# Pinning the early steps of a weight conversion to program order on ScalarE and VectorE

## The chip, the cores and the metric

The kernel runs on one core of a Trainium2 chip, as one launch. The metric is the device time of that launch in microseconds (us), the median of several executions.

## The reference

Sliding-window attention with sinks (2 batches, 8 heads, 768 positions, head size 64), followed by two feed-forward blocks over the 1536 tokens, each with d_model 512 and d_ff 2048. Only the activations differ. The weights of both blocks are 64-bit floats.

```
scores = where(is_sink | in_window, scale * q @ k.T, -1e9)      # 4 sinks, window 128
a = exp(scores - max); a = a / (sum(a) + 1e-9);  x = a @ v      # per batch and head
h = x @ w_in;  g = where(h >= 1, h, where(h <= -1, 0, (h + 1)**2 / 4));  x = g @ w_out
h = x @ w2_in; g = h * clip(h + 3, 0, 6) / 6;                   return g @ w2_out
```

## The kernel before

The program has an attention part and then, for each feed-forward block m, a first half over 16 d_ff tiles and a second half over the held activations.

**Attention.** `pairs` runs over four groups of query blocks (`GROUPS`) and four head pairs, so there are 16 pairs. Pairs 0 to 3 take four query blocks of 128 rows each, pairs 4 to 7 two, pairs 8 to 11 two (blocks 0 and 1 of the second batch), pairs 12 to 15 four. A unit is one query block of one pair; `score` makes its scores on TensorE (L310), VectorE adds the mask and finds the row minimum of the negated scores (L317), ScalarE takes exponentials (L336), VectorE makes the reciprocal of the sum (L328, L329), and GpSimd scales the two rows of probabilities (L331, two instructions a unit). `turn` transposes them on TensorE (L371, L372) and ScalarE or VectorE copies them out of PSUM (L353, L355). `sinks` does the same for the sink columns (L383), and `mix` multiplies by v (L408) once a pair, writing the feed-forward's input as a high and a low part (`xh`, `xl`).

**Weights.** `load_w` brings a weight tile of 128 x 512 doubles (512 KB) into one of four `raw` buffers by a DMA on SyncE (L162). Tiles are named by block, kind and d_ff tile: raw0i0 is w_in of block 0, tile 0; raw0o1 is w_out, tile 1. `take_weight` calls `take`, which calls `narrow` to make 32-bit floats in a tile w32 of the two halves of each double, and then `split` into a high and a low part (`wi`, `wo`). The steps of `narrow`:

- the high word without its sign, on ScalarE (L176) or VectorE (L174), whichever the planner `Balance` picks
- a clamp on VectorE (L179)
- the sign of the high word, in place in raw, on VectorE (L180)
- shift and join, on VectorE (L181)
- the low word to a float, in place in raw, on ScalarE (L184)
- one slot later, the sum of both on VectorE (L186)

Two slots later the high part is made (L134 on ScalarE or L136 on VectorE), then the low part on VectorE (L141). L174 or L176, L180 and L184 read nothing but what the DMA brought; the others read a step before them. `load_weights` issues the next load when a tile has been taken, three slots later, and that load waits for its raw buffer.

**Order.** TensorE and SyncE run in the order of the program text (`manual_schedule`). For ScalarE, VectorE and GpSimd the compiler's scheduler, which simulates a timeline, chooses the order in which instructions stand on each engine; on the chip each engine then takes them strictly in that order, waiting on semaphores. The program text loads the first four weight tiles half way through the attention's steps and takes raw0i0, raw0o0 and raw0i1 24, 14 and 6 steps before its end; all others are taken in the feed-forward part.

**Feed-forward, first half.** For each d_ff tile, `h_group` does 12 matmuls for each of three token chunks (L534) and `y_group` 12 for chunk 0 of the tile before (L564). `activate` works on chunk 0 at once: r on ScalarE (L511), then two steps on VectorE (L512, L513), then gh (L134) and gl (L141). Chunks 1 and 2 are held as copies `hs` (L134). PSUM has four `ps_h` buffers.

Of the kernel before, what the change touches and what calls it, by code (L numbers as in the profile page):

```python
# [11 lines left out]
U32 = mybir.dt.uint32  # L12
AF = mybir.ActivationFunctionType
ALU = mybir.AluOpType
# [51 lines left out]
def f32(ap):  # L66
    return ap.bitcast(F32)
# [3 lines left out]
def sink_attention_moe_moe_kernel(  # L71
# [14 lines left out]
    nc = tc.nc  # L86
# [27 lines left out]
    def defer(fn, slots=1):  # L114
        waiting.append((clock[0] + slots, fn))
# [14 lines left out]
    def high(dst, src, n, psum=False):  # L130

        e = bal.pick(act=(143 if psum else 190) + n / 1.2, dve=(140 + n / 0.96) if psum else (150 + n / 1.92))
        if e == "act":
            nc.scalar.activation(out=dst, in_=src, func=AF.Copy)  # L134
        else:
            nc.vector.tensor_copy(out=dst, in_=src)  # L136

    def low(dst, src, hi, n):

        bal.add("dve", 150 + n / 0.96)  # L140
        nc.vector.tensor_tensor(out=dst, in0=src, in1=f32(hi), op=ALU.subtract)  # L141
# [23 lines left out]
            nc.sync.dma_start(out=t, in_=src)  # L165
        raw[m, which, fc] = t

    def narrow(t, dst):

        lo, hi = t[:, :, 0], t[:, :, 1]  # L170
        c = dst.bitcast(I32)
        n = c.shape[1]
        if bal.pick(dve=150 + n / 1.92, act=150 + n / 1.2) == "dve":
            nc.vector.tensor_scalar(out=c, in0=hi, scalar1=0x7FFFFFFF, scalar2=None, op0=ALU.bitwise_and)  # L174
        else:
            nc.scalar.activation(out=f32(c), in_=f32(hi), func=AF.Abs)  # L176
        bal.add("dve", 3 * 150 + 2 * n / 1.92 + n / 0.96)
        bal.add("act", 150 + n / 1.2)
        nc.vector.tensor_scalar(out=f32(c), in0=f32(c), scalar1=F64_LOW, scalar2=F64_HIGH, op0=ALU.max, op1=ALU.min)  # L179
        nc.vector.tensor_scalar(out=hi, in0=hi, scalar1=-(1 << 31), scalar2=None, op0=ALU.bitwise_and)  # L180
        nc.vector.scalar_tensor_tensor(  # L181
            out=c, in0=c, scalar=3, in1=hi, op0=ALU.logical_shift_left, op1=ALU.bitwise_xor
        )
        nc.scalar.activation(out=f32(lo), in_=lo.bitcast(U32), func=AF.Copy, scale=2.0 ** -51, bias=2.0)  # L184
        bal.add("dve", 160 + 1.3 * n)
        defer(lambda: nc.vector.tensor_tensor(out=c, in0=c, in1=lo, op=ALU.add))  # L186

    def take(m, which, fc):

        t = raw.pop((m, which, fc))  # L190
        if which == "i":
            w = wi_p.tile([P, 2, DM], F32R, tag="wi", name=f"wi{m}")
            hi, lo = w[:, 0, :], w[:, 1, :]
            wi[m, fc] = (hi.rearrange("p (k f) -> p k f", f=P), lo.rearrange("p (k f) -> p k f", f=P))
        else:
            w = wo_tile(m, fc)
            hi, lo = w[:, 0, :], w[:, 1, :]

        def split(src):
            high(hi, src, DM)  # L200
            defer(lambda: low(lo, src, hi, DM))
            if which == "o":
                defer(lambda: nc.sync.dma_start(out=f32(wo_d[m][fc]), in_=f32(w.rearrange("p a f -> p (a f)"))), 4)

        if wide:
            t32 = raw_p.tile([P, DM], F32, tag="w32", name="w32", bufs=3)
            narrow(t, t32)
            defer(lambda: split(t32), 2)
        else:
            split(t)  # L210

    def wo_tile(m, fc):
        wo[m, fc] = wo_p.tile([P, 2, DM], F32R, tag="wo", name=f"wo{m}")
        return wo[m, fc]
# [372 lines left out]
    def take_weight(m, which, fc):  # L587
        if taken[0] < len(queue) and queue[taken[0]] == (m, which, fc):
            take(m, which, fc)
            taken[0] += 1  # L590
            defer(load_weights, 3)
# [3 lines left out]
    with tc.manual_schedule(engines={mybir.EngineType.PE, mybir.EngineType.SP}):  # L595
# [28 lines left out]
        for m in range(2):  # L624
# [19 lines left out]
            for n, (_, fc, c) in enumerate(first):  # L644
# [3 lines left out]
                if n + 2 < len(first):  # L648
                    t = held.pop(first[n + 2])
# [51 lines left out]
```

## Time and profile before

| what | us |
|---|---|
| median of 3 runs (654.04 to 656.28) | 655.56 |
| the profiled execution, its own time | 655.16 |
| its span in the trace | 653.4 |
| TensorE busy | 630.7 |
| VectorE busy | 423.2 |
| ScalarE busy | 328.2 |
| GpSimd busy | 91.5 |

The span runs from the first to the last instruction; the time of a launch has about 1.8 us around it. A matmul is pipelined and its end is modelled, so TensorE's busy time also covers stretches in which it is not at its peak. An engine's idle time is shown with what ended it.

### The profile page before, as it was taken

The numbers are of one execution on the slowest core, as the hardware profiler recorded it, in microseconds if no ns is written. First come the engines' busy times: TensorE is split into PE (matmuls) and PEld (weight loads), VectorE is DVE, ScalarE is ACT, GpSimd is POOL, SyncE is SP. The second block draws the span as 40 slices with busy tenths as digits, with TensorE's granted clock in tenths as the row PEclk, the third lists the DMA queues.
The fourth block names the chain that finished last, engine by engine and source line by source line (L and its number), as shares of the span: only waits on it lengthen the run. The fifth ranks groups of instructions, "written<-read, shape, count | busy, mean of one in ns | idle before, by whom it ended". The sixth has DMA issues, their size and how long they took to land.

```text
span 653.4 us, 8514 instructions
## 1 busy us (share of the span) xinstructions
PE 630.7 (97%) x3008; PEld 493.6 (76%) x3008; DVE 423.2 (65%) x953; ACT 328.2 (50%) x669; POOL 91.5 (14%) x115
## 2 busy tenths in 40 slices
PE   7997797899999999999999999999999999999997
PEld 4554454588888887888888888888888888888886
DVE  4778888856647567539995597565668302994443
ACT  5777679655455445337663486455533223850001
POOL 7896687200000000000000000000000000000000
PEclk9999799899999999999999999999999999999999
DMA  4237257734453344102223575445451010523203
GB/s 129 88 115 247 70 167 233 229 107 141 129 161 129 115 144 128 65 32 97 98 96 118 174 236 182 162 129 161 129 158 68 34 64 1 192 98 96 97 32 130
DMA packets 32330, 81.38 MB, mean 125 GB/s; under 512 B 3056, under 2 KB 12320, under 8 KB 32288
## 3 DMA queue, kind: packets, MB, share of 16 engines
q1 hardware_dynamic: 32288, 80.84, 38.1%
q8 instruction: 24, 0.39, 0.3%
q14 instruction: 18, 0.15, 0.1%
HBM read 60.91 MB, written 19.92 MB: 124 GB/s over the span
## 4 chain that ended last, share of the span: by engine, by line
PE 72%; DVE 10%; DMA 9%; ACT 6%; issue 2%; POOL 1%; SPq 0%; ACTq 0%; POOLq 0%; DVEq 0%
PE ps_y L564 36%; PE ps_h L534 28%; DMA raw0o<-moe_w_out_dram 6%; PE ps_v L408 3%; PE ps_s L310 3%; DVE w L186 2%; DVE w L181 2%; DMA raw0i<-moe_w_in_dram 2%; ACT p L336 1%; PE ps_t L371 1%; ACT w L176 1%; ACT raw0o L184 1%; DVE w L179 1%; PE ps_t L372 1%; DVE r L512 1%
## 5 line engine op out<-in xcount | busy, mean ns | idle before, releaser
L534 PE MATMUL ps_h<-xh,wi 128*128 128x512 f32 x768 | 242.1, 390 | 0.0
L564 PE MATMUL ps_y<-gh,wo 128*128 128x512 f32 x768 | 241.6, 389 | 0.0
L534 PEld LDWEIGHTS ps_h<-xh,wi 128*128 128x128 f32 x768 | 144.5, 188 | 30.3 <-issue 0.3
L564 PEld LDWEIGHTS ps_y<-gh,wo 128*128 128x128 f32 x768 | 144.1, 188 | 29.9
L564 PE MATMUL ps_y<-gl,wo 128*128 128x512 f32 x384 | 149.6, 390 | 0.6 <-DVE gl L141 0.6
L534 PE MATMUL ps_h<-xl,wi 128*128 128x512 f32 x384 | 149.6, 390 | 0.0
L331 POOL TENSOR_SCALAR p<-p,sm 128x260 f32<-128x260 f32 (+2 forms) x96 | 88.1, 938 | 25.7 <-DVE sm L329 8.6
L564 PEld LDWEIGHTS ps_y<-gl,wo 128*128 128x128 f32 x384 | 72.1, 188 | 16.2 <-DVE gl L141 1.3
L534 PEld LDWEIGHTS ps_h<-xl,wi 128*128 128x128 f32 x384 | 72.2, 188 | 15.0
L179 DVE TENSOR_SCALAR w<-w 128x512 f32<-128x512 f32 x64 | 27.7, 433 | 43.9 <-ACT w L176 42.9
L134 ACT ACTIVATE hs<-ps_h 128x512 f32<-128x512 f32 x64 | 37.5, 589 | 36.4 <-PE ps_h L534 36.3
L336 ACT ACTIVATE p<-p,nm 128x260 f32<-128x260 f32 (+2 forms) x96 | 46.3, 483 | 15.0 <-DVE nm L317 11.4
L141 DVE TENSOR_TENSOR gl<-hs,gh 128x512 fp32r<-128x512 f32 x64 | 44.0, 688 | 12.7 <-ACT gh L134 11.9
L310 PE MATMUL ps_s<-kraw,qraw 64*128 64x260 f32 (+2 forms) x192 | 37.8, 469 | 7.8 <-DMA kraw<-k_dram 4.4
L512 DVE SCALAR_TENSOR_TENSOR r<-r 128x512 f32<-128x512 f32 x48 | 32.3, 685 | 15.6 <-ACT r L511 15.4
L141 DVE TENSOR_TENSOR wi<-w,wi 128x512 fp32r<-128x512 f32 x32 | 22.1, 690 | 30.6 <-ACT wi L134 29.6
L516 DVE SCALAR_TENSOR_TENSOR ps_h<-r,ps_h 128x512 f32<-128x512 f32 x16 | 11.1, 694 | 46.2 <-ACT r L515 46.2
L317 DVE CUSTOM_DVE_ANT_0 p<-ps_s,mask 128x260 f32<-128x260 f32 (+2 forms) x96 | 35.7, 396 | 7.7 <-PE ps_s L310 7.0
L134 ACT ACTIVATE gh<-ps_h 128x512 fp32r<-128x512 f32 x32 | 19.2, 598 | 33.6 <-DVE ps_h L513 21.7
L134 ACT ACTIVATE gh<-hs 128x512 fp32r<-128x512 f32 x35 | 22.0, 629 | 26.0 <-PE ps_y L564 24.8
L572 ACT ACTIVATE o<-ps_y 128x512 f32<-128x512 f32 x6 | 3.6, 596 | 62.5 <-PE ps_y L564 62.5
L136 DVE CAST gh<-hs 128x512 fp32r<-128x512 f32 x29 | 12.3, 426 | 32.8 <-PE ps_y L564 32.7
(72 smaller groups left out, 688.7 us busy)
## 6 DMA issues: line engine op xcount, KB each, us to landing
wo_d<-wo SPq DMA_DIRECT2D x32, 512.0 KB, 5.0
wo<-wo_d SPq DMA_DIRECT2D x32, 512.0 KB, 3.2
raw0i<-moe_w_in_dram SPq DMA_DIRECT2D x16, 512.0 KB, 3.4
raw0o<-moe_w_out_dram SPq DMA_DIRECT2D x16, 512.0 KB, 5.1
raw1i<-moe_w_in_dram SPq DMA_DIRECT2D x16, 512.0 KB, 3.4
raw1o<-moe_w_out_dram SPq DMA_DIRECT2D x16, 512.0 KB, 4.1
out_dram<-o SPq DMA_DIRECT2D x12, 256.0 KB, 2.2
qraw<-q_dram SPq DMA_DIRECT2D x8, 256.0 KB, 2.8
```

The lines of the kernel that those rows point to most:

```text
L134: nc.scalar.activation(out=dst, in_=src, func=AF.Copy)
L141: nc.vector.tensor_tensor(out=dst, in0=src, in1=f32(hi), op=ALU.subtract)
L179: nc.vector.tensor_scalar(out=f32(c), in0=f32(c), scalar1=F64_LOW, scalar2=F64_HIGH, op0=ALU.max, op1=ALU.min)
L181: nc.vector.scalar_tensor_tensor(out=c, in0=c, scalar=3, in1=hi, op0=ALU.logical_shift_left, op1=ALU.bitwise_xor)
L310: nc.tensor.matmul(banks[e], tq[rows, u * P:(u + 1) * P], tk[rows, c0:c0 + w], start=True, stop=True)
L317: nc.vector.tensor_tensor_reduce(out=p[:, e, :], in0=banks[e], in1=masks[min(i, 2)], scale=-SCALE, scalar=BIG, op0=ALU.add, op1=ALU.min, a ...
L331: nc.gpsimd.tensor_scalar_mul(out=p[:, e, :], in0=p[:, e, :], scalar1=sm[:, e:e + 1])
L336: nc.scalar.activation(out=p[:, e, :], in_=p[:, e, :], func=AF.Exp, scale=-1.0, bias=nm[:, e:e + 1], accum_out=sm[:, e:e + 1],)
L408: nc.tensor.matmul(ps[e * D:(e + 1) * D, u0 * P:u1 * P], l, r, start=n == 0, stop=n == len(ops[0]) - 1)
L512: nc.vector.scalar_tensor_tensor(out=r, in0=r, scalar=1.0, in1=r, op0=ALU.min, op1=ALU.mult)
L534: nc.tensor.matmul(ps, w[:, kc, :], x[:, kc, :], start=i == 0, stop=i == len(ops) - 1)
L564: nc.tensor.matmul(ys[dm], a[:, cs], b, start=fc == 0 and i == 0, stop=last and i == 2)
```

## The change

`narrow` gets a third argument. For block 0 and d_ff tiles 0 to 2, the three steps that depend on the load alone are handed to `keep_in_program_order`, which adds an edge in the scheduler's graph from the instruction that was traced just before on the same engine: the step must stand behind it. The edge is of issue order only; no wait on a semaphore is added. No instruction is added or removed, and the planner's picks of engine stay as they are.

```diff
-    def narrow(t, dst):
+    def narrow(t, dst, keep):
+
+        def place(ins):
+            if keep:
+                tc.keep_in_program_order(ins)
 
         lo, hi = t[:, :, 0], t[:, :, 1]
...
         if bal.pick(dve=150 + n / 1.92, act=150 + n / 1.2) == "dve":
-            nc.vector.tensor_scalar(out=c, in0=hi, scalar1=0x7FFFFFFF, scalar2=None, op0=ALU.bitwise_and)
+            place(nc.vector.tensor_scalar(out=c, in0=hi, scalar1=0x7FFFFFFF, scalar2=None, op0=ALU.bitwise_and))
         else:
-            nc.scalar.activation(out=f32(c), in_=f32(hi), func=AF.Abs)
+            place(nc.scalar.activation(out=f32(c), in_=f32(hi), func=AF.Abs))
...
-        nc.vector.tensor_scalar(out=hi, in0=hi, scalar1=-(1 << 31), scalar2=None, op0=ALU.bitwise_and)
+        place(nc.vector.tensor_scalar(out=hi, in0=hi, scalar1=-(1 << 31), scalar2=None, op0=ALU.bitwise_and))
...
-        nc.scalar.activation(out=f32(lo), in_=lo.bitcast(U32), func=AF.Copy, scale=2.0 ** -51, bias=2.0)
+        place(nc.scalar.activation(out=f32(lo), in_=lo.bitcast(U32), func=AF.Copy, scale=2.0 ** -51, bias=2.0))
...
-            narrow(t, t32)
+            narrow(t, t32, m == 0 and fc < 3)
```

The order of TensorE, SyncE and GpSimd is the same in both programs. After the change all lines of the program from `narrow` on stand four to five lines further down (L184 is L188, L511 is L515).

First place: ScalarE in pair 8, just after the first four weight loads have been issued. The names p, pt, pts and ps_t belong to attention, raw0i0 and raw0o0 are weight tiles. Before:

```order
L353 ACTIVATE pt_877<-ps_t_925 128x2x256
L184 ACTIVATE raw0i0_913<-raw0i0_913 128x512
L353 ACTIVATE pt_952<-ps_t_954 128x2x128
L336 ACTIVATE p_941,sm_943<-p_941,nm_942 128x256 x2
L336 ACTIVATE p_966,sm_968<-p_966,nm_967 128x128
L176 ACTIVATE w32_1486<-raw0o0_915 128x512
L184 ACTIVATE raw0o0_915<-raw0o0_915 128x512
```

Now:

```order
L357 ACTIVATE pt_877<-ps_t_925 128x2x256
L357 ACTIVATE pt_952<-ps_t_954 128x2x128
L340 ACTIVATE p_941,sm_943<-p_941,nm_942 128x256 x2
L340 ACTIVATE p_966,sm_968<-p_966,nm_967 128x128 x2
L357 ACTIVATE pt_952<-ps_t_990 128x2x256
```

The three conversion steps that stood between attention's instructions are gone from here; raw0i0's now stands in pair 13.

Second place: VectorE in the same pair. Before:

```order
L328 TENSOR_SCALAR sm_943<-sm_943 128x2
L181 SCALAR_TENSOR_TENSOR w32_1365<-w32_1365,raw0i0_913 128x512
L329 RECIPROCAL sm_943<-sm_943 128x2
L136 CAST xh0_1_773<-ps_v_973 128x256
L186 ISA w32_1365<-raw0i0_913,w32_1365 128x1024
L179 TENSOR_SCALAR w32_1486<-w32_1486 128x512
L180 TENSOR_SCALAR raw0o0_915<-raw0o0_915 128x512
L317 ISA p_1000,nm_1001<-ps_s_996,mask1_126 128x256
```

Now:

```order
L332 TENSOR_SCALAR sm_943<-sm_943 128x2
L333 RECIPROCAL sm_943<-sm_943 128x2
L136 CAST xh0_1_773<-ps_v_973 128x256
L332 TENSOR_SCALAR sm_968<-sm_968 128x2
L141 TENSOR_TENSOR xl0_1_774<-ps_v_973,xh0_1_773 128x256
L333 RECIPROCAL sm_968<-sm_968 128x2
L321 ISA p_1000,nm_1001<-ps_s_996,mask1_126 128x256
```

The steps of w32_1365 (raw0i0) and w32_1486 (raw0o0) have left the row between a sum and its reciprocal.

Third place: VectorE at the seam to the feed-forward part, from the last pair's split (xl0_2) to the first activation (r_1649). Before:

```order
L186 ISA w32_1952<-raw0i5_1797,w32_1952 128x1024
L141 TENSOR_TENSOR wo0_1911<-w32_1912,wo0_1911 128x512
L136 CAST xh0_2_1327<-ps_v_1617 128x512
L179 TENSOR_SCALAR w32_2000<-w32_2000 128x512
L180 TENSOR_SCALAR raw0o5_1842<-raw0o5_1842 128x512
L141 TENSOR_TENSOR xl0_2_1328<-ps_v_1617,xh0_2_1327 128x512
L181 SCALAR_TENSOR_TENSOR w32_2000<-w32_2000,raw0o5_1842 128x512
L186 ISA w32_2000<-raw0o5_1842,w32_2000 128x1024
L512 SCALAR_TENSOR_TENSOR r_1649<-r_1649 128x512
```

Now:

```order
L190 ISA w32_1582<-raw0i1_917,w32_1582 128x1024
L141 TENSOR_TENSOR wi0_1581<-w32_1582,wi0_1581 128x512
L136 CAST xh0_2_1327<-ps_v_1617 128x512
L141 TENSOR_TENSOR xl0_2_1328<-ps_v_1617,xh0_2_1327 128x512
L516 SCALAR_TENSOR_TENSOR r_1649<-r_1649 128x512
L517 TENSOR_TENSOR ps_h_1636<-ps_h_1636,r_1649 128x512
L141 TENSOR_TENSOR gl_1651<-ps_h_1636,gh_1650 128x512
L183 TENSOR_SCALAR w32_1658<-w32_1658 128x512
L184 TENSOR_SCALAR raw0o1_919<-raw0o1_919 128x512
```

Before, twelve tiles (raw0i0 to raw0o5) are through L186 ahead of the first activation; now three are (raw0i0, raw0o0, raw0i1), and raw0o1, raw0i2 and the rest follow it.

## Rows read from the trace of the kernel before

**Rows 1.** Stretches: length, busy PE, PEld, DVE, ACT, POOL, then clock, DMA share, GB/s.

```profile
5.00:57.00 52.00, 51.93 (x356) 30.29 (x356) 39.02 (x186) 38.71 (x130) 43.85 (x52) 1.00 0.35 103
57.00:125.40 68.40, 54.62 (x349) 30.11 (x347) 58.76 (x201) 53.46 (x146) 44.26 (x45) 0.88 0.61 196
125.40:299.00 173.60, 173.01 (x761) 142.67 (x760) 105.51 (x185) 84.03 (x144) 0.00 (x0) 1.00 0.37 118
66.00:75.00 9.00, 5.68 (x34) 2.94 (x31) 8.85 (x33) 5.27 (x18) 4.35 (x5) 0.86 0.39 120
```

**Rows 2.** Waits of TensorE, 126 us to the end: total us, times, longest.

```profile
PE ps_y L564 <- DVE gl L141: 0.6, 1, 0.6
```

**Rows 3.** Timeline of ScalarE: start, us, instruction, in brackets idle before and releaser.

```profile
58.87 0.71 ACT L184 ACTIVATE raw0i<-raw0i 128x512 f32<-128x512 uint32 x1 [1.80 <-DMA raw0i<-moe_w_in_dram]
```

**Rows 4.** Timeline of TensorE, 64 to 126 us: three of its waits, and the seam.

```profile
64.79 0.56 PE L310 MATMUL ps_s<-kraw,qraw 64*128 64x128 f32 x4 [3.37 <-DVE sm L328]
...
111.06 1.07 PE L408 MATMUL ps_v<-pts,vs 4*64 4x512 f32 x4 [2.44 <-ACT pts L353]
...
121.39 1.07 PE L408 MATMUL ps_v<-pts,vs 4*64 4x512 f32 x4 [1.76 <-ACT pts L353]
...
125.36 0.80 PE L534 MATMUL ps_h<-xh,wi 128*128 128x512 f32 x1
```

**Rows 5.** Timeline of TensorE: first matmuls of the mix of pairs 0, 3, 4 and 7.

```profile
18.39 0.43 PE L408 MATMUL ps_v<-pts,vs 4*64 4x256 f32 x2
...
40.47 0.43 PE L408 MATMUL ps_v<-pts,vs 4*64 4x256 f32 x2
...
45.60 0.43 PE L408 MATMUL ps_v<-pts,vs 4*64 4x256 f32 x2
...
58.17 0.43 PE L408 MATMUL ps_v<-pts,vs 4*64 4x256 f32 x2
```

**Rows 6.** Groups by shape on GpSimd, 5 to 57 us: count, busy us, mean ns, idle before.

```profile
L331 POOL TENSOR_SCALAR p<-p,sm 128x260 f32<-128x260 f32 x32 | 29.3, 939 | 2.0 <-ACT p L336 1.1 <-DVE sm L329 0.8
L331 POOL TENSOR_SCALAR p<-p,sm 128x256 f32<-128x256 f32 x10 | 9.1, 926 | 3.9 <-ACT p L336 3.5 <-DVE sm L329 0.4
L331 POOL TENSOR_SCALAR p<-p,sm 128x128 f32<-128x128 f32 x10 | 5.9, 606 | 3.4 <-DVE sm L329 3.4
```

**Rows 7.** Groups of conversion steps on VectorE and ScalarE, 57 to 125.4 us.

```profile
L179 DVE TENSOR_SCALAR w<-w 128x512 f32<-128x512 f32 x11 | 5.1, 464 | 1.1 <-ACT w L176 1.1
L186 DVE CUSTOM_DVE_ANT_0 w<-raw0i,w 128x1024 uint16<-128x1024 uint16 x6 | 4.1, 682 | 0.0
L181 DVE SCALAR_TENSOR_TENSOR w<-w,raw0i 128x512 int32<-128x512 int32 x6 | 4.1, 682 | 0.0
L141 DVE TENSOR_TENSOR wi<-w,wi 128x512 fp32r<-128x512 f32 x4 | 2.7, 680 | 0.0
...
L184 ACT ACTIVATE raw0i<-raw0i 128x512 f32<-128x512 uint32 x7 | 4.7, 678 | 3.4 <-DMA raw0i<-moe_w_in_dram 1.8 <-DVE w L186 1.6
L134 ACT ACTIVATE wi<-w 128x512 fp32r<-128x512 f32 x4 | 2.5, 617 | 1.2 <-DVE w L186 1.2
```

**Rows 8.** The chain of waits: one load, and TensorE over one d_ff tile.

```profile
100.55 4.13 DMA raw0o<-moe_w_out_dram
...
388.40 10.88 PE ps_h L534 x48
```

**Rows 9.** Groups on VectorE, 126 to 299 us: activation and clamp.

```profile
L512 DVE SCALAR_TENSOR_TENSOR r<-r 128x512 f32<-128x512 f32 x21 | 14.3, 688 | 15.6 <-ACT r L511 15.4
...
L179 DVE TENSOR_SCALAR w<-w 128x512 f32<-128x512 f32 x25 | 10.7, 427 | 25.0 <-ACT w L176 24.1
```

**Rows 10.** The groups of rows 6 in 57 to 125.4 us.

```profile
L331 POOL TENSOR_SCALAR p<-p,sm 128x260 f32<-128x260 f32 x32 | 32.2, 1025 | 6.9 <-DVE sm L328 4.1 <-ACT p L336 2.1 <-PE ps_t L372 0.6
L331 POOL TENSOR_SCALAR p<-p,sm 128x256 f32<-128x256 f32 x7 | 7.2, 1034 | 7.1 <-DVE sm L329 3.7 <-ACT w L176 3.4
L331 POOL TENSOR_SCALAR p<-p,sm 128x128 f32<-128x128 f32 x6 | 5.5, 932 | 2.5 <-DVE nm L317 2.2 <-DVE sm L329 0.4
```

## The prediction

> **What bounds the kernel now.** I read the busy time by stretch first, then the waits of TensorE, then its timeline. From 125.4 to 299 us, the first half of the first feed-forward block, TensorE is busy for 173.01 of 173.60 us [rows 1], and from 126 us to the end it waits for 0.6 us in one place [rows 2]. So what lies behind the first product at 125.36 us [rows 4] is bound by TensorE, and only the start of that part can move the end. In the attention part the two halves differ. From 5 to 57 us TensorE is busy for 51.93 of 52 us at clock 1.00. From 57 to 125.4 us it is busy for 54.62 of 68.40 us, with about as many matmuls (349 after 356), at a mean granted clock of 0.88 of 2.4 GHz, while VectorE goes from 39.02 busy in 52 us to 58.76 in 68.4, and to 8.85 of 9 from 66 to 75 us [rows 1].
>
> The reader is to see two things behind that. ScalarE meets a conversion step of raw0i0 before the load has landed and stands for 1.80 us with attention's copies and exponentials behind it [rows 3]. More important, the steps of eleven tiles (L179 x11 [rows 7]) stand between attention's own steps on VectorE and ScalarE, and TensorE then waits for sums, copies and sink columns: 3.37, 2.44 and 1.76 us in three places [rows 4].
>
> **What the change does, and the sum.** It adds no instruction. It moves conversion work of eight to nine tiles from attention's second half into the feed-forward part, where the order of the changed program has three tiles (raw0i0, raw0o0, raw0i1) ahead of the first activation and the program before has twelve. The edges are of issue order, so no semaphore wait is added; what can be new is a pinned step standing in front of others, which I come to below.
>
> Step 1, the pace of attention without conversions. Pairs of four query blocks go from mix to mix in (40.47 - 18.39) / 3 = 7.36 us, pairs of two in (58.17 - 45.60) / 3 = 4.19 us [rows 5]. From the mix of pair 7 (58.17) to that of pair 15 (121.39 [rows 4]) lie four pairs of either kind. At the early pace they take 4 x 7.36 + 4 x 4.19 = 46.2 us; they take 63.2. The excess is 17.0 us, with the half-clock stretches in it, since these follow TensorE's waits.
>
> Two things make 46.2 uncertain. Pairs 8 to 11 have narrow blocks: GpSimd needs 2 x (0.606 + 0.926) = 3.06 us for one, and pairs 12 to 15 have only wide ones, 8 x 0.939 = 7.51 us [rows 6]. With GpSimd as the sole limit the eight pairs take 42.3 us and the excess is 20.9. An early pair of four blocks costs GpSimd 2 x (0.606 + 0.926 + 2 x 0.939) = 6.82 us and takes 7.36, a factor of 1.08; 7.51 x 1.08 = 8.1 us for the late ones, with 4.19 for the others, makes 49.2 us and an excess of 14.0. I keep 46.2: it is the direct row, the four weight loads that start at half way stay where they are, beside the loads of the first narrow pairs, and the two deviations have opposite signs.
>
> Step 2, what stays. Three tiles are still converted inside the last pairs, so their cost returns. Eleven tiles go with an excess of 17.0 us: 1.55 us each, 4.6 for three. The ends: nothing, where their steps fall into gaps; or all of their VectorE time in series, 2 x 0.464 + 0.682 + 0.682 + 0.680 = 2.97 us a tile (L180 priced as L179 [rows 7]), 8.9 for three. I take 4.6, because VectorE has 13 of 52 us free at the early pace [rows 1], too little to hide all and enough to hide half.
>
> Step 3, the seam. From the last mix to the first product pass 3.97 us [rows 4]. ScalarE's copies of the sink columns before it still stand behind a conversion in the changed order (raw0i1's), so I leave wait, seam and its clock as they are: 0, where removing the wait of 1.76 us would be the other end.
>
> Step 4, the conversions in the feed-forward part: 0. Nine tiles x 2.97 us = 27 us of VectorE and 9 x (2 x 0.678 + 0.617), about 17.8, of ScalarE (L176 priced as L184), go beside 173.6 us in which VectorE has 105.51 and ScalarE 84.03 busy [rows 1]. The cover is TensorE's own work, 10.88 us for one d_ff tile [rows 8]. It holds as long as weights come in time. The tightest is raw0i2: its first product comes 10.88 x 36/48 + 10.88 = 19.0 us after the start. Ahead of its low part stand one group of products (2.7 us), ScalarE's r and gh (0.7 and 0.6, the size of L184 and L134 [rows 7]), three steps of the activation at 0.688 [rows 9], the VectorE steps of raw0o1 and raw0i2 (2 x 2.97), two steps of the next activation (1.4), and for each tile two ScalarE steps that VectorE waits for (2 x 1.3): 2.7 + 1.3 + 2.1 + 5.9 + 1.4 + 2.6 = 16.0. Slack 3 us; each further d_ff tile adds 10.88 of time against some 6 of VectorE work for its two weights, so the lead should grow.
>
> Sum: 17.0 - 4.6 = 12.4 us gained. The profiled execution took 655.16 us (span 653.4), so 655.16 - 12.4 = **642.8 us**. The median of the runs shown, 655.56, lies 0.4 above that execution; I make no correction for it.
>
> **Weighed against a rule.** GpSimd's scaling takes 939, 926 and 606 ns early [rows 6] and 1025, 1034 and 932 ns in the half with the conversions [rows 10]; 32 x 0.086 + 7 x 0.108 + 6 x 0.326 = 5.5 us. VectorE's clamp takes 464 ns there [rows 7] and 427 where GpSimd is idle [rows 9]. So the two engines hold each other up by fractions of an instruction, half a microsecond a tile, and this is inside the 1.55. The Trainium skill (SBUF — State Buffer, section "SBUF: two separate sides") says that the shared port pair of VectorE and GpSimd is an exclusive lock for a whole instruction, and the loser blocks fully. Taken at its word it speaks against the change as made, which moves the three tiles from narrow pairs, where GpSimd idles, into the wide pairs, where it runs almost without gaps; by the rule I would expect the saving of rival A, by the rows the sum above.
>
> **Rivals.**
>
> A, a whole scaling lost per step: three tiles bring six instructions of the L179 and L180 kind, a first step on VectorE and a cast, eight in all; each held for one scaling of 0.939 us makes 7.5 us on top, and the gain is 4.9: 650.3 us. For it: the longer rows of GpSimd. Against it: the clamp's mean rose by 0.04 us, not by 0.9.
>
> B, the three tiles in series with the tail: every step of theirs, 2.97 on VectorE and 1.9 on ScalarE, lies on attention's path. 3 x 4.9 = 14.7 back, a gain of 2.3: 652.9 us. For it: strict order on both engines and the waits at 111 and 121 us behind ScalarE's copies. Against: eleven tiles cost 17.0 before, not 54.
>
> C, slower: the feed-forward part starves. ScalarE's unpinned step on raw0i3 now stands directly ahead of the first activation r; its load starts only when raw0i1 is through, near the seam, and takes 4.13 us [rows 8]. Behind it stand r, the activation and the next conversions. The first y needs gh and gl after four groups, 10.88 us, and its chain takes about 6.1, so a landing up to some 5 us late costs nothing. If each of the first five d_ff tiles exposed a whole load, 20.7 us would be lost: 655.16 - 12.4 + 20.7 = 663.5 us. It turns the sign once three of them (12.4 / 4.13) are exposed. Against it: VectorE and ScalarE have room, and all raw buffers are freed sooner than they are needed.
>
> D, no change: attention's second half is held up by transfers, not by order. The DMA share is 0.61 there against 0.35 [rows 1], and the loads stay on SyncE in the same order. Then about 655. Against: the waits end on VectorE, ScalarE and GpSimd, none on a load of q, k or v.
>
> **How the numbers follow.** Forecast 0.80, A 0.05, B 0.06, C 0.05, D 0.04. The forecast's own range: free tiles at the direct pace, 655.16 - 17.0 = 638.2; tiles paid in full on VectorE, 17.0 - 8.9 = 8.1 gained, 647.0; the slow pace with the usual price, 14.0 - 4.6 = 9.4, 645.7; slow and full together 650.1. I set 638 to 650.5, which takes in A and leaves B, C and D out, 0.15. A measurement of this kernel can tell about 0.3%, 2 us. Faster: forecast, A and B, 0.91; same: D, 0.04; slower: C, 0.05.
>
> **What would show it.** Right: the first product at 112 to 114 us; TensorE's waits of 3.37 and 2.44 us gone and clock 1.00 from 57 to 90 us; three clamps (L183) before the first product, not eleven; TensorE still without waits behind it. Step 1 is wrong if the mixes of pairs 8 to 11 stay over 5 us apart; step 2 if the last four pairs take over 9.5 us each; step 4 if TensorE waits for wi or gl within 40 us of its first product. A time over 653.6 would refute the whole.

## The result, and the profile after

The changed kernel takes 648.31 us (median of 4 runs, 646.67 to 649.26), the kernel before beside it 655.07 (654.04 to 656.28): a ratio of 0.9893 with a 95% interval of 0.9866 to 0.9921, 6.8 us less. The forecast was 642.8 in 638.0 to 650.5: the direction held, the gain is 6.8 of 12.4 us. The profiled execution took 648.49 us with a span of 646.7.

The busy time by stretch of the kernel after, cut at its own seam. The columns are those of [rows 1].

```profile
5.00:57.00 52.00, 51.95 (x366) 30.24 (x366) 40.08 (x190) 38.99 (x132) 45.02 (x54) 1.00 0.38 108
57.00:119.30 62.30, 54.03 (x339) 29.61 (x338) 38.93 (x160) 39.96 (x121) 39.11 (x43) 0.84 0.39 135
119.30:293.00 173.70, 173.70 (x766) 143.81 (x765) 123.45 (x225) 97.72 (x169) 0.00 (x0) 1.00 0.45 146
```

VectorE has gone from 58.76 to 38.93 busy in attention's second half and from 105.51 to 123.45 in the feed-forward stretch, and TensorE does not mind: it is busy for all of the 173.70 us. Attention's second half ends 6.1 us earlier, 1.2 of which is an earlier start (below). But its mean clock is 0.84, no better than the 0.88 before, and TensorE still waits in four kinds of places. The waits of TensorE, 57 to 126 us (total, times, longest):

```profile
PE ps_s L314 <- DMA kraw<-k_dram: 3.4, 1, 3.4
PE ps_v L412 <- ACT pts L357: 1.8, 2, 1.7
PE ps_t L375 <- POOL p L335: 1.7, 3, 0.6
PE ps_v L412 <- DVE pts L359: 1.3, 1, 1.3
```

The groups on VectorE from 57 to 119.3 us have three clamps where [rows 7] had eleven:

```profile
L183 DVE TENSOR_SCALAR w<-w 128x512 f32<-128x512 f32 x3 | 1.6, 532 | 0.4 <-ACT w L180 0.4
```

Where the 6.7 us between the two spans (653.4 and 646.7) come from, read from the first matmul of each mix and the first product on TensorE's timeline, in us:

| stretch | before | after | difference | forecast for after |
|---|---|---|---|---|
| start to the mix of pair 7 | 58.17 | 56.93 | -1.24 | as before |
| pairs 8 to 11 (narrow) | 25.23 | 20.39 | -4.84 | 16.8 |
| pairs 12 to 15 (wide) | 37.99 | 36.49 | -1.50 | 34.0 |
| seam, last mix to first product | 3.97 | 5.51 | +1.54 | as before |
| first product to the end | 528.03 | 527.34 | -0.69 | as before |

The first row is no effect of the change: the order up to there is the same, and from the mix of pair 0 to that of pair 7 both take 39.8 us; one execution began later. So what the change itself did between pair 7 and the first product is 67.19 - 62.40 = 4.8 us in these two executions, against 12.4 forecast. The gap of 7.6 is 3.6 in the narrow pairs, 2.5 in the wide ones and 1.5 in the seam.

Of the 4.84 us in the narrow pairs, pair 10 gave 4.16 (8.49 us before, 4.33 after) and pair 11 gave 1.67, while pairs 8 and 9 took 1.0 more. Pair 10 is where TensorE waited for GpSimd's scaling before the change, for 3.9 us in three places, the first of them the longest; after the change it doesn't wait there:

```profile
73.67 0.33 PE L371 MATMUL ps_t<-ident,p 128*128 128x128 f32 x1 [2.82 <-POOL p L331]
```

Two lines name suspects. In the chain of waits of the kernel after, 55 to 75 us, the wait in pair 8 is a load of k:

```profile
57.41 5.99 DMA kraw<-k_dram
63.40 0.14 issue
63.54 0.80 PE ps_s L314 x4
```

It is 128 KB and takes 5.99 us; SyncE issued it just behind the four weight loads of 512 KB, and the first experiment tests whether that is why. The wait of 3.37 us that the trace before put down to a sum on VectorE [rows 4] has the same place, and its size is 3.35 now. And in the timeline of ScalarE after, the high part of raw0i1 stands ahead of the last two copies:

```profile
112.18 0.63 ACT L134 ACTIVATE wi<-w 128x512 fp32r<-128x512 f32 x1 [1.54 <-DVE w L190]
112.72 0.58 ACT L357 ACTIVATE pt<-ps_t 128x512 f32<-128x512 f32 x1
113.19 0.57 ACT L357 ACTIVATE pts<-ps_k 4x512 f32<-4x512 f32 x1
```

ScalarE waits 1.54 us for VectorE's sum for raw0i1 (L190) with attention's last copies behind it; the last mix starts at 113.81, and the whole seam runs at half clock:

```profile
113.81:119.33 5.52, 5.51 (x25) 2.44 (x25) 0.00 (x0) 0.67 (x1) 0.00 (x0) 0.50 0.18 68
```

### The profile page after: what moved, and what is told of

Same layout as the page of the kernel before. It is cut to its first block, busy times and chain, and to the rows that moved or that the text cites. A ratio compares the mean times of both kernels' runs of the same rounds, so it can differ in the third digit from the quotient of the medians.

```text
span 646.7 us, 8523 instructions
## 1 busy us (share of the span) xinstructions
PE 629.7 (97%) x3008; PEld 493.4 (76%) x3008; DVE 421.4 (65%) x953; ACT 327.8 (51%) x669; POOL 87.5 (14%) x115
## 4 chain that ended last, share of the span: by engine, by line
PE 93%; ACT 3%; DMA 1%; POOL 1%; DVE 1%; issue 1%; SPq 0%; DVEq 0%; ACTq 0%; POOLq 0%
PE ps_h L538 40%; PE ps_y L568 40%; PE ps_v L412 5%; PE ps_s L314 4%; PE ps_t L375 2%; DMA kraw<-k_dram 1%; PE ps_t L376 1%; ACT p L340 1%; POOL p L335 1%; PE ps_k L387 1%; ACT pt L357 0%; ACT pts L357 0%; ACT wi L134 0%; ACT xh L134 0%; ACT w L180 0%
## 5 line engine op out<-in xcount | busy, mean ns | idle before, releaser
L335 POOL TENSOR_SCALAR p<-p,sm 128x260 f32<-128x260 f32 (+2 forms) x96 | 84.1, 895 | 23.2 <-DVE sm L333 10.6
```

The source lines that it names most:

```text
L335: nc.gpsimd.tensor_scalar_mul(out=p[:, e, :], in0=p[:, e, :], scalar1=sm[:, e:e + 1])
```

## Experiments

Each kernel was run beside the kernel before. The times are medians, and the ratios, with their intervals, are to the runs of the kernel before beside them. The stretches in the table are read as above, from each kernel's one profiled execution; where two kernels have the same instructions in pairs 8 to 11, those pairs still differ by up to 3.3 us (last section).

| kernel | median us | ratio (95%) | pairs 8-11 | pairs 12-15 | seam |
|---|---|---|---|---|---|
| the change | 648.31 | 0.9893 (0.9866-0.9921) | 20.39 | 36.49 | 5.51 |
| loads apart | 643.27 | 0.9806 (0.9783-0.9829) | 14.28 | 36.24 | 5.27 |
| three tiles not converted | 642.36 | 0.9784 (0.9761-0.9807) | 17.79 | 33.86 | 2.89 |
| tiles taken earlier | 643.74 | 0.9824 (0.9797-0.985) | 17.78 | 36.97 | 2.89 |
| before, loads apart | 654.05 | 0.998 (0.996-0.9999) | 21.11 | 39.50 | 5.51 |
| loads apart and tiles earlier | 641.89 | 0.9795 (0.977-0.9821) | 14.66 | 36.43 | 2.89 |
| pins on ScalarE alone | 648.00 | 0.9892 (0.9864-0.992) | 17.30 | 36.84 | 5.51 |
| pins on VectorE alone | 659.25 | 1.0054 (1.003-1.0078) | 19.21 | 47.38 | 5.51 |
| pins for tile 0 alone | 659.51 | 1.0071 (1.0045-1.0096) | 20.16 | 44.85 | 5.48 |
| pins for all tiles of block 0 | 649.79 | 0.9889 (0.9861-0.9917) | 21.07 | 36.47 | 5.37 |
| both edits, loads and tiles still earlier | 640.45 | 0.9758 (0.9731-0.9785) | 16.83 | 35.68 | 2.89 |

**Weight loads apart.** Whether the remaining wait is the load's.

```diff
-                    if n == len(steps) // 2:
-                        load_weights()
+                    if n - len(steps) // 2 in (0, 8, 16, 24):
+                        load_w(*queue[issued[0]])
+                        issued[0] += 1
```

> The changed kernel, with the first four weight loads issued one at a time, 8 steps apart, instead of together half way through attention. Transfer theory: the wait of 3.35 us in pair 8 that the change left is the k load (128 KB, 5.99 us) queued behind those four loads, and the half clock in pairs 8 and 9 follows it. Then the wait falls under 0.5 us, pairs 8 and 9 take together about 8.5 us instead of 12.8, and the time falls by 3.5 to 4.5 us to about 644. Rival, own pace: the first narrow pairs of the second batch are slow by themselves; then a wait of 3 us stays with another releaser and the time stays within 0.7 us of the changed kernel (648.3).

Measured: 643.27 us, ratio 0.9806, so 0.9% below the change. The wait in pair 8 is gone; one of 1.3 us for a k load shows up in pair 9. Pairs 8 and 9 take 8.0 us, not 12.8. The stretches show the clock with it, first of the change, then with loads apart:

```profile
57.00:66.00 9.00, 5.64 (x40) 3.30 (x40) 4.04 (x25) 4.51 (x19) 5.03 (x7) 0.80 0.88 332
66.00:75.00 9.00, 9.00 (x45) 4.83 (x45) 5.13 (x25) 4.94 (x17) 4.82 (x6) 0.63 0.38 120
```

```profile
57.00:66.00 9.00, 7.71 (x62) 4.49 (x63) 6.30 (x35) 6.43 (x24) 6.94 (x10) 1.00 0.78 244
66.00:75.00 9.00, 9.00 (x71) 5.30 (x67) 7.00 (x35) 5.81 (x20) 7.92 (x9) 1.00 0.75 239
```

TensorE counts as busy for 9.00 us in both second rows, with 45 matmuls in the one and 71 in the other: at the lower clock less work fills the stretch. The narrow pairs' own pace is 14.3 us for four, with the wait of 1.3 us still in it, near the 12.2 that GpSimd alone asks for by [rows 6] and far from the 16.8 that I took from earlier pairs. The transfer theory holds.

**The same edit in the kernel before.** Whether the wait before the change was the load's too.

> The kernel before, with the first four weight loads 8 steps apart. Transfer theory: the wait of 3.37 us in pair 8 before the change, which the trace put down to a VectorE sum, was the k load's as well; pair 8 falls from 7.1 to under 5.2 us and the time by 2 to 4 us, to 651 to 653. Rival, conversions: before the change the wait came from the conversion steps on VectorE; pair 8 stays over 6.5 us and the time within 1 us of 655.1.

Pair 8 falls from 7.12 to 3.82 us, with VectorE as crowded as before (8.05 busy of 9 from 57 to 66 us, 7.93 before) and raw0i0's steps still among attention's. So the wait of 3.37 us in [rows 4] was the load's, and the trace named the wrong releaser. The time falls by less than forecast, 0.2% (0.01 to 0.4). The narrow pairs gain 4.1 us, but the wide pairs lose 1.5 and the seam 1.5: the conversions stay in attention, and nine clamps, not seven, now stand between the mix of pair 11 and the first product.

```profile
57.00:66.00 9.00, 7.14 (x56) 4.10 (x54) 8.05 (x35) 6.64 (x22) 4.23 (x7) 1.00 0.77 224
66.00:75.00 9.00, 6.36 (x34) 3.15 (x34) 8.15 (x31) 5.67 (x18) 6.73 (x7) 0.80 0.53 170
```

**Three tiles not converted.** What step 2 costs.

```diff
-            narrow(t, t32, m == 0 and fc < 3)
-            defer(lambda: split(t32), 2)
+            if m == 0 and (fc == 0 or (fc == 1 and which == "i")):
+                defer(lambda: split(f32(t[:, :, 1])), 2)
+            else:
+                narrow(t, t32, m == 0 and fc < 3)
+                defer(lambda: split(t32), 2)
```

> The changed kernel without the steps L178 to L190 for raw0i0, raw0o0 and raw0i1: their high words go straight into the split, so these three tiles hold other numbers. It measures what the three conversions cost inside the last pairs. Conversion theory: they cost the 2.5 us by which pairs 12 to 15 exceed 34.0 and the price of 4.6 us in it, and the seam loses its wait of 1.65 us; first product 4 to 7 us earlier, time 641 to 644. Rival, GpSimd: the wide pairs take 8.5 to 9.5 us by themselves; then first product under 1.5 us earlier, time 647 or more.

The wide pairs fall from 36.49 to 33.86 us and the seam from 5.51 to 2.89: 2.6 + 2.6 = 5.2 us for the three conversions. (Their high and low parts are still made, but in this kernel they stand in pairs 8 to 11, so the wide pairs are free of all three tiles.) Almost all of the cost in the pairs belongs to the last tile: pair 15 takes 6.27 us instead of 9.40, while pairs 12 to 14 take 27.59 without the steps and 27.09 with them. In the seam the same 25 matmuls run in 2.89 us at clock 1.00, where the change needs 5.52 at 0.50:

```profile
109.78:112.67 2.89, 2.89 (x25) 1.48 (x25) 0.00 (x0) 0.00 (x0) 0.00 (x0) 1.00 0.02 6
```

The wide pairs' own pace is thus 8.5 us in the mean, not 7.36, from unequal pairs: 8.64, 10.33, 8.62 and 6.27. The time, ratio 0.9784, is 1.1% or 7 us below the change; 2.6 of that is pairs 8 to 11 (20.39 and 17.79 us), which in this kernel hold more steps than in the change, not fewer; the last section comes back to it.

**The three tiles taken earlier.** Whether the work costs, or its place.

```diff
-                    if n == len(steps) - 24:
+                    if n == len(steps) - 36:
...
-                    if n == len(steps) - 14:
+                    if n == len(steps) - 28:
...
-                    if n == len(steps) - 6:
+                    if n == len(steps) - 20:
```

> The changed kernel with the three tiles taken 36, 28 and 20 steps before attention's end instead of 24, 14 and 6. Conversion theory with the place deciding: the wait of 1.65 us before the last mix and the half clock of the seam come from raw0i1's steps standing ahead of the last sink copies on ScalarE; the seam falls from 5.5 to about 3.5 us, the pairs before keep their sum, time 1.5 to 2.5 us lower, about 646.3. Rival, the work decides: the same steps cost the same in earlier pairs, the sum from pair 12 to the first product stays within 0.7 us, time 647.6 to 649.

The seam is 2.89 us, as without the steps: the wait before the last mix is 0.68 us and the seam's clock is 1.00. Pairs 12 to 15 keep their sum (36.97 after 36.49). So the three tiles' work cost 2.6 to 3.1 us within the wide pairs at either place, and the place of the last, in front of the last copies, cost 2.6 more in the seam. The time went down further than forecast (643.74, not 646.3), again by 2.6 in pairs 8 to 11.

```profile
112.37 1.07 PE L412 MATMUL ps_v<-pts,vs 4*64 4x512 f32 x4 [0.68 <-ACT pts L357]
113.38 1.95 PE L412 MATMUL ps_v<-pt,vraw 128*64 128x128 f32 x20
115.26 0.50 PE L538 MATMUL ps_h<-xh,wi 128*128 128x512 f32 x1
```

**Both edits.**

> The changed kernel with both edits: weight loads 8 steps apart, and the three tiles taken 36, 28 and 20 steps before attention's end. If the load wait and the seam are two separate remainders of the change, pairs 8 to 11 take about 14.3 us as with the spread loads alone, the seam 2.9 us as with the earlier places alone, and the time is 640 to 641.5. Rival, the remainders share a cause (what is won early is lost again in the wide pairs 12 to 15): the time stays at 643 to 644.

The parts do what each did alone (14.66, 36.43, 2.89), and the profiled execution took 640.3 us, but the median is 641.89, just above the forecast, with an interval that overlaps that of the loads alone. It beats the change clearly; that it beats the loads alone is not shown.

**Pins on one engine alone.** Which of the pins does the work. The first kernel drops `place` from VectorE's two steps, the second from ScalarE's two.

```diff
-            place(nc.vector.tensor_scalar(out=c, in0=hi, scalar1=0x7FFFFFFF, scalar2=None, op0=ALU.bitwise_and))
+            nc.vector.tensor_scalar(out=c, in0=hi, scalar1=0x7FFFFFFF, scalar2=None, op0=ALU.bitwise_and)
...
-        place(nc.vector.tensor_scalar(out=hi, in0=hi, scalar1=-(1 << 31), scalar2=None, op0=ALU.bitwise_and))
+        nc.vector.tensor_scalar(out=hi, in0=hi, scalar1=-(1 << 31), scalar2=None, op0=ALU.bitwise_and)
```

> The changed kernel with the pins on ScalarE's steps alone (high word without sign, low word to a float); VectorE's first steps and sign step are free again. Theory that ScalarE's early steps lead the crowding, since every VectorE step but the sign reads one of them: the conversions stay at the end of attention, time as the change, 647.5 to 649.5. Rival, VectorE's sign step does it: the time returns to within 2 us of before, 653 or more.

```diff
-            place(nc.scalar.activation(out=f32(c), in_=f32(hi), func=AF.Abs))
+            nc.scalar.activation(out=f32(c), in_=f32(hi), func=AF.Abs)
...
-        place(nc.scalar.activation(out=f32(lo), in_=lo.bitcast(U32), func=AF.Copy, scale=2.0 ** -51, bias=2.0))
+        nc.scalar.activation(out=f32(lo), in_=lo.bitcast(U32), func=AF.Copy, scale=2.0 ** -51, bias=2.0)
```

> The counterpart: pins on VectorE's steps alone, ScalarE's free. Theory that ScalarE's early steps lead the crowding: more than three tiles are converted before the first product, with their VectorE work in the last pairs, and the time is 652 to 657. Rival, either pin is enough: 647.5 to 649.5.

ScalarE's pins alone give the whole change (0.9892). VectorE's alone give a kernel slower than before (1.0054), and slower than the 652 to 657 expected: the narrow pairs are free of conversion steps on VectorE, though not of four on ScalarE, but eleven tiles are converted in the last four pairs, which take 47.4 us. The groups on VectorE from 76 to 128.9 us and TensorE's waits from 77 to 129 us of that kernel:

```profile
L183 DVE TENSOR_SCALAR w<-w 128x512 f32<-128x512 f32 x11 | 5.1, 467 | 0.0
```

```profile
PE ps_t L375 <- DVE xl L141: 5.3, 1, 5.3
PE ps_t L375 <- POOL p L335: 2.9, 4, 1.8
```

So the gain of the change is not that conversions leave the narrow pairs, but that most of them leave attention.

**Pins for d_ff tile 0 alone.** The condition becomes `m == 0 and fc < 1`.

> The changed kernel with pins for d_ff tile 0 alone instead of 0 to 2. Crowding theory, by the number of tiles ahead of the first product: tiles from raw0i1 on float up into the last two pairs, these take together over 4 us more than the 18.2 of the change, and the time is 652 to 658, the first two tiles' gain in the narrow pairs given back. Rival, only the place of the first tile matters (its steps stood in front of a load that had not landed): time 647 to 649.5.

659.51 us, slower than before and than expected. The narrow pairs take as long as in the change; nine clamps stand between 77 us and the first product, and pairs 14 and 15 take 11.69 and 14.82 us. Mixes wait 3.34 us for a copy (before pair 14's) and 1.81 (before pair 15's). From the mix of pair 7 to the first product pass 70.49 us, 3.3 more than before: moved within attention, the conversions give back what the narrow pairs gained, and more. That is not all of it. From the first product to the end pass 532.02 us, 4.0 more than before, with 2.3 us of waits of TensorE for gh and gl, the kind of wait that rival C feared; what held gh and gl up here was not followed:

```profile
PE ps_y L568 <- ACT gh L134: 1.4, 1, 1.4
PE ps_y L568 <- DVE gl L141: 0.9, 2, 0.7
```

The waits of TensorE for copies within attention:

```profile
107.07 1.97 PE L412 MATMUL ps_v<-pts,vs 4*64 4x512 f32 x4 [3.34 <-ACT pts L357]
...
121.89 1.97 PE L412 MATMUL ps_v<-pts,vs 4*64 4x512 f32 x4 [1.81 <-ACT pts L357]
```

**Pins for all tiles of block 0.** The condition becomes `m == 0`.

> The changed kernel with pins for all d_ff tiles of block 0, so that no later tile's ScalarE step stands ahead of an activation it could hold up. Theory: TensorE never waits in the feed-forward part after the change, so these unpinned steps cost nothing, and the time stays at 647.5 to 649.5. Rival, the starving of the feed-forward part: unpinned steps delay the first activations somewhere; pinning them gains 1 us or more, 647 or less. A third way: the pins keep the weights from running ahead of TensorE, and waits appear in the feed-forward part, 650 or more.

Ratio 0.9889, the same as the change within the intervals; the median of 649.79 stands beside 657.34 for the kernel before, so only the ratio counts. The first product to the end takes 529.24 us, 1.9 more than in the change, with 1.7 us of waits for gl in the feed-forward part. Pinning them gained nothing, and in the change TensorE waits nowhere behind the first product: the unpinned steps ahead of the first activation, the start of rival C, held nothing up.

**Both edits, still earlier.**

```diff
+                    if n - len(steps) // 2 in (-8, 0, 8, 16):
+                        load_w(*queue[issued[0]])
+                        issued[0] += 1
...
+                    if n == len(steps) - 46:
...
+                    if n == len(steps) - 36:
...
+                    if n == len(steps) - 24:
```

> The changed kernel with the weight loads one at a time at 8 steps before, at, and 8 and 16 steps after half way, and the three tiles taken 46, 36 and 24 steps before attention's end. If the wide pairs have room for the conversions when they are spread further, pairs 12 to 15 fall from the 36.4 of the version with both edits towards the 33.9 without conversions and the time to 639 to 641. Rival, the steps cost the same wherever they stand: 641 to 643.

640.45 us, ratio 0.9758: the lowest ratio of the study, 2.4% below before. The wide pairs fall to 35.68 us, less than hoped; the narrow ones rise to 16.83, with a wait of 2.2 us for a k load and raw0i0's first steps now among them. That it beats the version before it is not shown, since the intervals overlap.

## Why the prediction was right, and where its size failed

**What bounds the kernel: right.** Behind the first product TensorE waits nowhere after the change, and what the change itself did lies between pair 7 and the first product. Conversions do crowd attention there: with eleven or nine tiles of them in the last four pairs (pins on VectorE, pins for tile 0) those pairs take 47.4 and 44.9 us, with three 36.5.

**The signs set down beforehand** are mixed. The three clamps came, and no waits stood behind the first product. But the first product came at 119.33 us, not at 112 to 114; the wait of 3.37 us stayed, with a mean clock of 0.80 and 0.63 in the two stretches from 57 to 75 us; and pairs 8 and 9, 7.34 and 5.47 us long, are the sign that was named for step 1 being wrong. That the time lies in the range is luck in part: the range's upper end was worked out from a slow pace with a full price for three tiles, neither of which came, and the wait that took the time up there has no term in it.

**Where the 7.6 us went.** An estimate from one profile of each kernel, with the narrow pairs' own pace from loads apart (14.28 us for four) and the wide pairs' from three tiles not converted (33.86), against 16.8 and 29.4 in the prediction: narrow pace -2.5, the load's wait and the clock behind it +6.1, wide pace +4.4, the three tiles in the wide pairs -2.0, seam +1.5.

**Step 1, the excess of 17.0 us: the failing term.** The pace of 46.2 us was nearly right as a sum: 14.28 + 33.86 = 48.1, inside the bounds of 42.3 to 49.2, with narrow pairs faster and wide ones slower than taken. What failed is that all of the excess was put down to the conversions. The wait of 3.37 us "for sums" was a load's, which the change does not touch. In pairs 8 to 11 it cost 20.39 - 14.28 = 6.1 us in the profiled execution of the change, and 17.78 - 14.28 = 3.5 where the clock came back sooner. The prediction has a sentence on the four loads beside the first narrow pairs and used it only to leave the pace as it was. Rival D, transfers, was rejected because no wait ended on a load of q, k or v; the releaser named there was not the true one. The timeline of SyncE and the DMA view of the trace before would have shown it:

```profile
57.90 0.44 SPq L281 DMA_DIRECT2D kraw<-k_dram  x1
```

```profile
kraw<-k_dram SPq DMA_DIRECT2D x4, 128.0 KB, 6.8
```

The view has a landing for only one of these four loads of 128 KB, the one issued at 57.90 us: it took 6.8 us, twice the 3.2 that the same view gives for 328 KB, and so landed at 64.7, where TensorE's wait ended (64.79). VectorE's sum ended at that moment too. What the change did remove in the narrow pairs is another wait, for GpSimd's scaling in pair 10, which is not among the three that the prediction names.

**Step 2, 4.6 us for three tiles: too much for the pairs** (2.6 measured), and wrong as a price for each: at their places in the change, two cost nothing that can be seen and the last all. Its cost in the seam is on top.

**Step 3, the seam at 0: wrong by 1.5 us.** I wrote that ScalarE's last copies still stand behind a conversion, and left wait and clock as they were. The wait stayed (1.65 us after 1.76), but the clock did not: 0.50 through the whole seam, after 0.72 before, and the same seam takes 2.89 us at full clock.

**Step 4, the feed-forward part at 0: right.** It took 527.34 us after 528.03. With pins for tile 0 alone, where nine tiles stand ahead of the first product, it was not free (532.02).

**The rivals.** A gives 650.3 us, near the result, but not by its mechanism. GpSimd's wide scalings take 990 ns in the change and 937 without the three tiles' steps, 32 x 0.053 = 1.7 us, not 7.5; the three clamps take 532 ns in the mean after 427 in the feed-forward part [rows 9], 0.1 each. The Trainium skill's lock for a whole instruction (SBUF — State Buffer, "SBUF: two separate sides") agrees with the rows in that the two engines hold each other up; its price, estimated from the length of one scaling [rows 6], would be up to 0.94 us a step, and the mean of the rows shows a fraction of that. B fell too: the steps are not all in series. C did not occur in the change. D was true in part: in the kernel before, loads apart take 4.1 us off the narrow pairs, of which 3.0 come back in the wide pairs and the seam while the conversions stay.

## What to carry to other kernels

Before an excess is credited to one cause, look at each wait in it for a second releaser that ends at the same time. Here a small load that took longer than a large one was a load issued just behind others, whatever engine the trace named. Work that was moved away from one place of a crowded part came back in the next unless it left the part; count how many instances stand ahead of the seam in the new order. Here the last instance ahead of the seam cost most: 3.1 us in its pair, and 2.6 in the seam, which ran at half clock behind its wait.

## What the runs showed of the hardware that was not expected

The same order of instructions takes different times through the clock that follows a wait. In three kernels (the change, tiles earlier, all pins) TensorE, VectorE and ScalarE have the same instructions in the same order from the mix of pair 7 to that of pair 11, with the loads beside them, and those pairs took 20.39, 17.78 and 21.07 us, each after a wait of 3.3 to 3.7 us for the k load. Two others, with a few conversion steps in those pairs, took 17.79 (three tiles left out) and 17.30 (pins on ScalarE) after waits of 3.2 and 2.8 us. From 66 to 75 us the granted clock was 0.63 in the change and 0.92 with the tiles taken earlier, and TensorE ran 45 and 64 matmuls in the same 9 us:

```profile
66.00:75.00 9.00, 9.00 (x64) 5.18 (x62) 6.74 (x32) 6.78 (x23) 5.61 (x7) 0.92 0.39 119
```

So one wait of a little over 3 us had a price of 3.5 to 6.8 us, against the 14.28 of loads apart. Each kernel has one profile, so these runs do not show whether the clock's return goes with the kernel or with the execution. The median of tiles earlier lies 4.6 us below that of the change, and its seam and wide pairs explain 2.1 of that, so the sooner clock is hardly that of one execution alone. Why the clock comes back sooner is open.
